# Weight tiles on GpSimd's DMA queue, and a planner with new books for transfers

## The chip, the core and the metric

The kernel runs on one core of one Trainium2 chip. The metric is the device time of one execution in microseconds (us). The engines are named as in the profile: PE (TensorE, with PEld for its weight loads), DVE (VectorE), ACT (ScalarE), POOL (GpSimd) and SP (SyncE, which here only issues transfers).

## The reference

A delta-rule attention (4 batches, 8 heads, 768 positions, head size 48), and then a gated FFN over its output (3072 tokens of 384, inner size 1536), all in float32. The weights arrive as 8-byte floats.

```python
k_n = k / (np.linalg.norm(k, axis=-1, keepdims=True) + 1e-06)
for t in range(S):
    kt, vt, bt = (k_n[:, :, t], v[:, :, t], beta[:, :, t, None])
    y[:, :, t] = np.einsum('bhd,bhde->bhe', q[:, :, t], state)
    v_old = np.einsum('bhde,bhd->bhe', state, kt)
    state = state + bt[:, :, :, None] * np.einsum('bhd,bhe->bhde', kt, vt - v_old)
...
xn = x / np.sqrt(np.mean(x * x, axis=-1, keepdims=True) + 1e-06) * rms_g
g = xn @ w_gate
out = (g * (1.0 / (1.0 + np.exp(-g))) * (xn @ w_val)) @ w_out
```

## The kernel before, in words

The 768 positions are cut into 12 chunks of 64. For every chunk, `prep` works out what the chunk needs of k and beta alone, `recur` applies and updates the state and gives the chunk's 256 normalized tokens, and an FFN follows.

`prep(c)` normalizes k (`norms`: the squares' sum on DVE, its square root on POOL at L538), forms the products of keys on PE (L516), copies them negated, writes them to a DRAM scratch `dkk`, and reads them back in another layout as `at` (256 KB in two halves). A triangular solve follows on DVE: 15 steps of a multiply (L682) and a reduce (L688). Its result goes through the DRAM scratch `dx` to the tiles `mt`, `x2bd` and `m1bd`, from which two small merges on PE (L764, L788) make the chunk's inverse. For chunks 0 and 1, PE turns a part of it (L740), and ACT (L751) and DVE (L753) each copy one half into `m1bd`. There is one `at` tile, so a chunk's `at` is loaded only when the solve before has read it. In `recur(c)`, PE applies the inverse (L875), the scores (L889) and the state update (L926); POOL takes a root for the RMS norm (L976); PE transposes the tokens (L997) and ACT writes them to `xf` (L1001).

Chunks 0 and 1 use a plain FFN in two halves (L1064 up, L1046 down), chunks 2 to 11 one with fewer products (L1157 up, L1214 down), whose factors DVE works out from the weights (L1122, L1193).

The weights are 18 tiles of 768 KB. Each is loaded as raw 8-byte numbers into one of three `raw` buffers (in tile `more`). ACT splits it (L454, L455) into one of two scratch pairs, and DVE joins the parts (L456, L457) into float32 in `w_in` or `wo_sb`. The first nine tiles feed the first half of the plain FFN.

The order of the work is not written out by hand. Every piece is handed to a class `Plan` as an `Op`: engine, estimated duration, priority, what it reads and writes, PSUM banks that it takes or frees. `Plan.run` makes 60 rounds: `forward` lists the pieces by their earliest possible start, and by key among equals, and reckons when each ends; `backward` works out from the end how late each could start, and that is the next round's key, slightly shaken. The best round by the reckoned end is emitted, so each engine gets its instructions in that fixed order. In the first 70 us of the plan, gaps on PE are filled with matmuls on the identity (L1314), which compute nothing.

A transfer in the plan (`dma`, from L367, its queue chosen at L368) occupies its issuing engine for `dur`, then one common server for `work`, 0.9 us after the issue at the earliest, and its user may start 0.7 us after that. `after` gives a time before which the plan does not issue it: the first seven weight tiles have one each (7.5, 5.0, 19.2, 27.2, 24.5, 33.3, 47.0), the others 48.8; the beta loads 7.5; the chunk 1 `at` 41.2; q, k and v have their own. Nearly all transfers are issued by SP; for chunk 0 some of them by ACT. L369 is the line of every issue.

Of the kernel before, what the change touches and what calls it, by code (L numbers as in the profile page):

```python
# [18 lines left out]
C = 64  # L19
# [9 lines left out]
SHAKE = 0.12  # L29


class Op:
    def __init__(self, eng, dur, fn, prio, deps, lat, acquire, release, slack):
# [4 lines left out]
        self.ready, self.dma, self.ahead, self.work = 0.0, False, 0.0, 0.0  # L38

# [23 lines left out]
class Plan:  # L63
# [47 lines left out]
    def forward(self, banks, until):  # L111

        at = dict.fromkeys(ENGINES, 0.0)
# [9 lines left out]
        order, server, end_, mode = [], 0.0, 0.0, 0  # L123
        backlog = 0.0
        while len(order) < len(self.ops):
            best = None
            for e in ENGINES:
                for op in cand[e]:
                    s = max(op.at, at[e])
                    if op.port:  # L130
                        s = max(s, held["POOL" if e == "DVE" else "DVE"])
# [23 lines left out]
            end = s + op.dur  # L155
# [17 lines left out]
            if op.dma:  # L173
                server = max(end + 0.9, server) + op.work
                end = server
# [8 lines left out]
        return order  # L184

# [64 lines left out]
def kernel(  # L250
# [116 lines left out]
    def dma(dst, src, prio, r=(), w=(), work=0.3, dur=0.5, eng="SP", after=0.0):  # L367
        queue = nc.scalar if eng == "ACT" else nc.sync  # L368
        op = P.add(eng, dur, lambda: queue.dma_start(out=dst, in_=src), prio, r, w, lat=0.7)  # L369
        op.dma, op.work, op.ready = True, work, after  # L370
# [44 lines left out]
    def load_small():  # L415
        for i in range(8):
            src = beta.rearrange("b (y g) (c i t) -> i g (b y) c t", i=2, g=2, t=W)[i // 2 % 2, i % 2]
            dma(beta_b[16 * i : 16 * i + 16], src, 0.5, w=[("beta", i)], work=0.2, after=7.5)
        dma(g_sb, moe_rms_g.rearrange("(t p) -> p t", p=128), 1, w=["g"], after=8.0)
# [6 lines left out]
    def weights():  # L426
# [14 lines left out]
        for n, (dst, src, keys) in enumerate(todo):  # L441
# [4 lines left out]
            dma(rdst, src, (0.1 if n == 0 else 3 + 2 * n), w=[("raw", i)], dur=0.7, work=3.06, after=(7.5, 5.0, 19.2, 27.2, 24.5, 33.3, 47.0)[n] if n < 7 else 48.8)  # L446
# [18 lines left out]
    def load(c, what):  # L465
        t0 = c * C
        pk, pq, pv = ((-5, 1, 12), (5, 29, 36))[c] if c < 2 else (due(c, 150), due(c, 99), due(c, 70))
        if "q" in what and c > 1:
            for d, eh, g, th in itertools.product(range(2), repeat=4):
# [3 lines left out]
                dma(q2t[r0 : r0 + 32, :, g, th, 0 : e1 - e0], src, pq, w=[q2k[8 * d + 4 * eh + 2 * g + th]], work=0.2, after=53.2)  # L473
        for key, t, src, pr in (("k2", k2[c % NK], k, pk), ("q2", q2, q, pq)):
            for g in range(2):
# [4 lines left out]
                dma(dst, s, pr, w=[(key, c % NK, g)] if key == "k2" else q2k[8 * g : 8 * g + 8], dur=0.7, work=1.02, eng="ACT" if c == 0 and g and key == "k2" else "SP", after=((0.0, 1.4, 0.0), (8.6, 27.2, 0.0))[c]["kqv".index(key[0])] if c < 2 else 53.2)  # L480
        if "v" in what:
            for bb in range(2):
                s = v[2 * bb : 2 * bb + 2, :, t0 : t0 + C, :].rearrange("p h t e -> t (p h) e")
                dma(vt[64 * bb : 64 * bb + 64], s, pv, w=[("v", bb)], dur=0.85, work=1.02, after=(34.4, 41.2)[c] if c < 2 else 60.0)
# [865 lines left out]
```

## Time and profile before

| what | us |
|---|---|
| median of 3 runs (717.48 to 721.77) | 720.96 |
| the profiled execution | 718.33 |
| its span, first to last instruction | 716.6 |
| PE busy (98% of the span) | 700.2 |
| filler matmuls among it (L1314) | 56.6 |
| DVE busy (74%) | 533.4 |
| ACT busy (44%) | 314.0 |
| POOL busy (19%) | 137.5 |

The transfers moved 54.66 MB. Nearly all went through one hardware queue (q1, that of SP: 52.27 MB), a small part through q10 (0.92 MB). Shares of the chain that ended last: PE 77%, DVE 10%, DMA 5%, SP's issuing 4%.

In a row of a group, "x164 | 56.6, 498 | 1.4" reads: 164 instructions, busy 56.6 us, 498 ns each on average, 1.4 us of idle time of the engine ahead of them. In a row of a timeline, the first number is the start and the second the duration; an issue on SP ("SPq") is the time that the issue took, not the transfer. A row of transfers gives the size of each and the median time from issue to landing.

### The profile page before, as it was taken

The numbers are of one execution on the slowest core, as the hardware profiler recorded it, in microseconds if no ns is written. First come the engines' busy times: TensorE is split into PE (matmuls) and PEld (weight loads), VectorE is DVE, ScalarE is ACT, GpSimd is POOL, SyncE is SP. The second block draws the span as 40 slices with busy tenths as digits, with TensorE's granted clock in tenths as the row PEclk, the third lists the DMA queues.
The fourth block names the chain that finished last, engine by engine and source line by source line (L and its number), as shares of the span: only waits on it lengthen the run. The fifth ranks groups of instructions, "written<-read, shape, count | busy, mean of one in ns | idle before, by whom it ended". The sixth has DMA issues, their size and how long they took to land.

```text
span 716.6 us, 23156 instructions
## 1 busy us (share of the span) xinstructions
PE 700.2 (98%) x9940; PEld 631.0 (88%) x9940; DVE 533.4 (74%) x1115; ACT 314.0 (44%) x724; POOL 137.5 (19%) x140
## 2 busy tenths in 40 slices
PE   8999799999999999999999999989999999999997
PEld 6655676777879999999999999989999999999997
DVE  4799549999349959959869888569859838947363
ACT  5454855323314534544545336424535345236231
POOL 4200203103031231322134304032133112000000
PEclk9999999999999999999999999999999999999999
DMA  7977887351531452531541634421551350040000
GB/s 139 240 173 188 188 228 127 53 86 29 85 67 27 84 96 42 90 54 22 94 74 30 102 58 65 72 52 25 76 96 19 47 97 2 13 65 2 23 1 23
DMA packets 232790, 54.66 MB, mean 76 GB/s; under 512 B 221936, under 2 KB 225008, under 8 KB 232688
## 3 DMA queue, kind: packets, MB, share of 16 engines
q1 hardware_dynamic: 227840, 52.27, 38.3%
q8 instruction: 78, 1.28, 0.8%
q10 hardware_dynamic: 4848, 0.92, 0.7%
q14 instruction: 24, 0.20, 0.1%
HBM read 40.83 MB, written 12.32 MB: 74 GB/s over the span
## 4 chain that ended last, share of the span: by engine, by line
PE 77%; DVE 10%; DMA 5%; SPq 4%; issue 2%; ACT 1%; POOL 1%; DVEq 0%; POOLq 0%; ACTq 0%
PE bank L1157 35%; PE bank L1214 17%; PE bank L1064 7%; SPq L369 4%; PE bank L1046 3%; DVE acc L688 3%; PE bank L516 3%; PE bank L829 3%; DMA more<-in_moe_w_out_dram 2%; DVE acc L682 2%; PE bank L875 2%; PE bank L788 2%; PE bank L889 2%; DVE tmp L1167 1%; PE bank L493 1%
## 5 line engine op out<-in xcount | busy, mean ns | idle before, releaser
L1157 PE MATMUL bank<-xf,w_in 128*128 128x128 f32 x1440 | 181.1, 277 | 0.0
L1157 PEld LDWEIGHTS bank<-xf,w_in 128*128 128x128 f32 x1440 | 170.1, 192 | 2.0 <-issue 0.6
L1167 DVE TENSOR_TENSOR tmp<-tmp,bank 128x512 f32<-128x512 f32 x180 | 120.7, 682 | 66.1 <-PE bank L1157 58.0
L1157 PE MATMUL bank<-xf,more 128*128 128x128 f32 x960 | 126.2, 279 | 2.0 <-DVE tmp L1167 2.0
L1157 PEld LDWEIGHTS bank<-xf,more 128*128 128x128 f32 x960 | 116.0, 193 | 4.7 <-DVE tmp L1167 2.4
L1169 ACT COPY tmp<-bank 128x512 f32<-128x512 f32 x120 | 68.9, 585 | 104.8 <-PE bank L1157 80.8
L688 DVE TENSOR_REDUCE acc<-acc 128x30 f32<-128x90 f32 (+4 forms) x180 | 85.0, 472 | 6.2
L1173 ACT ACTIVATE tmp<-tmp 128x256 f32<-128x256 f32 x120 | 49.6, 416 | 89.1 <-DVE tmp L1167 89.0
L538 POOL TENSOR_TENSOR knrm<-ksum,half 128x16 f32<-128x16 f32 x12 | 35.3, 2943 | 212.1 <-DVE ksum L537 212.1
L682 DVE TENSOR_TENSOR acc<-acc,at 128x60 f32<-128x60 f32 (+4 forms) x180 | 62.8, 349 | 8.8 <-DMA out_dram<-tmp 3.4
L1214 PE MATMUL bank<-wo_sb,hf 128*128 128x192 f32 x360 | 63.7, 327 | 0.0
L1214 PEld LDWEIGHTS bank<-wo_sb,hf 128*128 128x128 f32 x360 | 58.3, 190 | 0.1
L1314 PE MATMUL bank<-ident 128*128 128x512 f32 (+2 forms) x164 | 56.6, 498 | 1.4 <-POOL ident masks.py:199 1.4
L1174 DVE TENSOR_TENSOR hf<-tmp 128x256 f32<-128x256 f32 x120 | 50.5, 437 | 7.7 <-ACT tmp L1173 7.2
L1314 PEld LDWEIGHTS bank<-ident 128*128 128x128 f32 x164 | 29.7, 200 | 27.0 <-issue 24.7
L635 POOL TENSOR_TENSOR at<-at,beta_b 128x1024 f32<-128x1024 f32 x8 | 18.9, 2358 | 121.3 <-DMA at<-dkk 63.1
L709 POOL COPY acc<-acc 128x128 f32<-128x128 f32 x40 | 20.1, 532 | 89.8 <-DVE acc L688 89.6
L1223 DVE TENSOR_TENSOR tmp<-tmp,bank 128x192 f32<-128x192 f32 x30 | 10.5, 351 | 33.2 <-PE bank L1214 33.2
L1064 PE MATMUL bank<-xf,w_in 128*128 128x256 f32 x144 | 33.6, 385 | 0.0
L1064 PE MATMUL bank<-xp,w_in 128*128 128x256 f32 x144 | 33.5, 384 | 0.0
L1046 PE MATMUL bank<-wo_sb,hf 128*128 128x384 f32 x96 | 33.0, 488 | 0.0
L1064 PEld LDWEIGHTS bank<-xf,w_in 128*128 128x128 f32 x144 | 26.7, 190 | 4.5 <-issue 0.4
(156 smaller groups left out, 1000.3 us busy)
## 6 DMA issues: line engine op xcount, KB each, us to landing
at<-dkk SPq DMA_DIRECT2D x23, 256.0 KB, 4.1
more<-in_moe_w_val_dram SPq DMA_DIRECT2D x6, 768.0 KB, 7.2
more<-in_moe_w_gate_dram SPq DMA_DIRECT2D x6, 768.0 KB, 7.8
more<-in_moe_w_out_dram SPq DMA_DIRECT2D x6, 768.0 KB, 8.9
vt<-in_v_dram SPq DMA_DIRECT2D x24, 192.0 KB, 4.3
out_dram<-tmp SPq DMA_DIRECT2D x48, 96.0 KB, 2.2
k<-in_k_dram SPq DMA_DIRECT2D x23, 192.0 KB, 3.9
mt<-dx SPq DMA_DIRECT2D x84, 32.0 KB, 2.1
```

The costliest lines, as they stand in the source:

```text
L538: P.add("POOL", 2.95, lambda: nc.gpsimd.tensor_tensor(out=knrm[i2], in0=ksum[i2], in1=half, op=ALU.pow), pn, r=[("ksum", i2), "half"], w=[ ...
L682: nc.vector.tensor_tensor(out=acc[:, 1:3, 0:n, j + 2 : W].rearrange("p a i t -> p i a t"), in0=acc[:, old, 0:n, j : j + 2, None].to_broadc ...
L688: nc.vector.tensor_reduce(out=acc[:, new, 0:n, j + 2 : W], in_=acc[:, lo : lo + 3, 0:n, j + 2 : W].rearrange("p a i t -> p i t a"), axis=A ...
L1046: nc.tensor.matmul(po[p].t[:, 0:DM], hf[:, spot(f), 128 * p : 128 * p + 128], wo_sb[:, spot(f)], start=(f == f0), stop=(f == f1 - 1), skip ...
L1064: nc.tensor.matmul(ps.t[:, TOK * side : TOK * side + TOK], w_in[:, side, h_, 3 * t + i_, n : n + 128], x_[:, 2 * t : 2 * t + 2].rearrange( ...
L1157: nc.tensor.matmul(g.t[:, 128 * z : 128 * z + 128], fac[:, side, 128 * f : 128 * f + 128], xf[:, xs], start=(begin and z == 0), stop=False ...
L1167: P.add("DVE", V(512), lambda t=t, g=g: nc.vector.tensor_tensor(out=t, in0=t, in1=g.t, op=ALU.add), -1, r=[g], w=[tk], last=g)
L1169: P.add("ACT", A(512), lambda t=t, g=g: nc.scalar.copy(t, g.t), -1, r=[g], w=[tk], last=g)
L1173: P.add("ACT", A(256), lambda t=t: nc.scalar.activation(out=t[:, 0:256], in_=t[:, 0:256], func=ACTF.Silu), -1, w=[tk])
L1174: P.add("DVE", V(256), lambda t=t, f0=f0, p=p: nc.vector.tensor_tensor(out=hf[:, spot(f0) : spot(f0) + 2, 128 * p : 128 * p + 128], in0=t[ ...
L1214: nc.tensor.matmul(g.t[:, 0:192], a_[:, f], b_[:, f], start=(begin and f == 0), stop=(f == 5), skip_group_check=True)
L1314: nc.tensor.matmul(warm[:, 0 : 128 * w_].rearrange("p (w n) -> p w n", n=128), ident, ident[:, None, :].to_broadcast([128, w_, 128]))
```

## The change

Three things change in `dma`, in its calls, and in `Plan`. The kernel's arithmetic, tiles and buffers stay.

1. The 18 weight loads are issued on POOL's queue, not on SP's.
2. All `after` times of transfers are gone. A load of q and k for chunks 2 and later, and of v for chunks 1 and later, is marked `hold`: the plan does not issue it more than 24 us before its key.
3. `forward` reckons otherwise. POOL's transfers have a server of their own, starting 1.08 us after the issue and landing 0.9 us after the server is done. Those of SP and ACT share the other one, 1.08 us after the start of the issue, and are stretched by up to 0.6 of their work while POOL's server is busy, which is pushed back as well. A transfer is not issued before the eighth one ahead of it on its kind of queue has landed. An issue on SP or ACT also ends only when its descriptors (`desc`) fit with those still under way into a room of 2330 (`room`). The estimates of `dur` and `work` are new throughout.

```diff
+RING, LANES, FIRST, LAND = 2330, 8, 1.08, 0.9
+HOLD = 24.0
...
                     s = max(op.at, at[e])
+                    if op.dma:
+                        s = max(s, (softly if op.soft else landed)[-LANES])
+                        if op.held:
+                            s = max(s, op.key - HOLD)
...
-            if op.dma:
-                server = max(end + 0.9, server) + op.work
-                end = server
+            if op.soft:
+                soft = max(end + FIRST, soft) + op.work
+                end = soft + LAND
+                softly.append(end)
+            elif op.dma:
+                end = self.room(sent, end, op.desc)
+                at[op.eng] = end
+                begun = max(server, s + FIRST)
+                work = op.work
+                if soft > begun:
+                    work += min(0.6 * op.work, soft - begun)
+                    soft += op.work
+                server = max(begun + work, end)
+                sent.append((begun, server, op.desc))
+                end = server + LAND
+                landed.append(end)
...
+    def room(self, sent, t, desc):
+
+        left = lambda t: sum(n if t <= a else n * (b - t) / (b - a) for a, b, n in sent[-24:] if b > t) + desc
+        if left(t) <= RING:
+            return t
+        lo, hi = t, max(b for a, b, n in sent[-24:])
+        for _ in range(12):
+            mid = (lo + hi) / 2
+            lo, hi = (mid, hi) if left(mid) > RING else (lo, mid)
+        return hi
...
-    def dma(dst, src, prio, r=(), w=(), work=0.3, dur=0.5, eng="SP", after=0.0):
-        queue = nc.scalar if eng == "ACT" else nc.sync
-        op = P.add(eng, dur, lambda: queue.dma_start(out=dst, in_=src), prio, r, w, lat=0.7)
-        op.dma, op.work, op.ready = True, work, after
+    def dma(dst, src, prio, r=(), w=(), work=0.2, dur=0.45, eng="SP", after=0.0, desc=256, hold=False):
+        queue = {"ACT": nc.scalar, "SP": nc.sync, "POOL": nc.gpsimd}[eng]
+        op = P.add(eng, dur, lambda: queue.dma_start(out=dst, in_=src), prio, r, w, lat=0.1)
+        op.dma, op.work, op.ready, op.desc, op.soft, op.held = True, work, after, desc, eng == "POOL", hold
+        op.port = False
...
-            dma(rdst, src, (0.1 if n == 0 else 3 + 2 * n), w=[("raw", i)], dur=0.7, work=3.06, after=(7.5, 5.0, 19.2, 27.2, 24.5, 33.3, 47.0)[n] if n < 7 else 48.8)
+            dma(rdst, src, (0.1 if n == 0 else 3 + 2 * n), w=[("raw", i)], dur=1.3, work=3.06, eng="POOL")
```

The other calls only lose `after` and get other estimates, for instance the two halves of `at`:

```diff
-                dk.rearrange("i g x j t -> (i g x) (j t)"), pd, r=dkeys, w=[("at", par)], dur=0.56, work=1.8, eng="SP" if par or c else "ACT", after=41.2 if c == 1 else 0.0)
+                dk.rearrange("i g x j t -> (i g x) (j t)"), pd, r=dkeys, w=[("at", par)], dur=0.5, work=1.42, desc=64, eng="SP" if par or c else "ACT")
```

## The prediction

> **What bounds the kernel now.** I read the page's first two parts, then the busy time by stretch, then in the first 90 us the chain of work that ended last, the timelines of PE, DVE, ACT and POOL, and the SP issues with their landings. The page first:
>
> ```profile
> PE 700.2 (98%) x9940; PEld 631.0 (88%) x9940; DVE 533.4 (74%) x1115; ACT 314.0 (44%) x724; POOL 137.5 (19%) x140
> ...
> L1314 PE MATMUL bank<-ident 128*128 128x512 f32 (+2 forms) x164 | 56.6, 498 | 1.4 <-POOL ident masks.py:199 1.4
> ...
> at<-dkk SPq DMA_DIRECT2D x23, 256.0 KB, 4.1
> ```
>
> PE is busy in 700.2 of 716.6 us, so 16.4 are idle; but 56.6 of the busy time is L1314, the filler matmuls on `ident` that compute nothing. So some 73 us hold no useful PE work, and all but some 9 of them lie in the first 90 us. The busy time by stretch says where:
>
> ```profile
> 60.00:70.00 10.00, 8.40 (x70) 5.35 (x69) 9.14 (x20) 5.81 (x10) 0.00 (x0) 0.86 0.71 146
> 70.00:80.00 10.00, 7.55 (x273) 7.01 (x272) 7.52 (x16) 8.15 (x24) 5.88 (x4) 0.84 0.89 215
> ...
> 280.00:330.00 50.00, 50.00 (x651) 48.62 (x652) 39.63 (x89) 22.77 (x55) 16.57 (x14) 1.00 0.34 60
> ...
> 430.00:480.00 50.00, 48.42 (x700) 46.63 (x698) 33.03 (x71) 23.99 (x58) 13.45 (x13) 1.00 0.39 67
> ```
>
> The columns are stretch, length, busy PE, PEld, DVE, ACT and POOL, then granted clock, DMA share and GB/s. From 230 to 680 us PE idles 0 to 1.58 us in 50, 3.3 in all; the end (680 to 717) adds 4.5. Past the start there is little to win. The start ends with the first useful FFN matmul (L1064), at 84.19 on PE's timeline. What it waits for, on the chain of work that ended last:
>
> ```profile
> 17.55 7.50 DMA at<-dkk
> ...
> 43.36 3.22 DMA dx<-wsum
> ...
> 64.60 0.28 DVE acc L688
> 64.88 0.32 DVE m1bd L753
> ```
>
> and on the timelines of ACT and DVE (start, duration):
>
> ```profile
> 54.96 0.73 ACT L751 COPY m1bd<-bank 32x256 f32<-32x256 f32 x2 [1.63 <-PE bank L740]
> ```
>
> ```profile
> 48.29 1.22 DVE L635 TENSOR_TENSOR at<-at,beta_b 128x1024 f32<-128x1024 f32 x1
> ...
> 64.79 0.84 DVE L753 COPY m1bd<-bank 32x256 f32<-32x256 f32 x2
> ```
>
> ACT copies its half of chunk 0's m1bd at 54.96; DVE copies the other half at 64.79, since chunk 1's whole solve (48.29 to 64.8) stands ahead of it in DVE's order. That is 9.8 us of the wait for the FFN, put there by the planner. The `at` load (17.55, 7.50 us against a median of 4.1) is the other visible stretch. On SP the weight loads are in the way:
>
> ```profile
> 31.54 4.79 SPq L369 DMA_DIRECT2D more<-in_moe_w_gate_dram  x1
> ...
> 57.14 4.75 SPq L369 DMA_DIRECT2D more<-in_moe_w_gate_dram  x1
> ```
>
> **The change part by part.** The profiled execution took 718.33 us (span 716.6, 1.73 around it); the median shown, 720.96, is 2.63 above. The sum goes against 718.33.
>
> *Eighteen weight issues leave SP.* Their durations on SP's timeline add up to 28.9 us, from 0.37 to 5.73 each. On SP they delayed others: chunk 1's dx was issued at 71.50, its mt only from 82.26. None of that ends PE's wait: with FFN work of chunk 0 at hand PE is busy from 84 to 114. What covers it is that first FFN half; without that cover chunk 1 would lead and the freed SP would gain more. Counted at 0.
>
> *The same issues land on POOL.* No DMA of POOL is in this trace. An issue is bounded by 0.37 (quickest on SP) and 2.94 (mean of L538, POOL's longest frequent instruction); I take the 1.3 that the diff books, which lies between. 18 x 1.3 = 23.4 us, beside 23.3 us of POOL work in the first 120 us: room enough on average. On the path lie L538 at 70.87 and the two L976 at 74.45 and 76.09, whose rs chunk 0's output waits for; three weight issues fell between 69 and 78 us. One issue ahead of rs costs 1.3, two 2.6, none 0. I take +1.3. An issue also waits until its `raw` buffer is free, with POOL's queue behind it: that is a rival.
>
> *`at` without a weight ahead on its own queue.* Its SP half took 7.50 behind a gate tile issued at 16.52. Its ACT half, issued at 17.46 with no weight on its queue, took 6.00 beside the same traffic. Best is the median 4.1 (-3.4); worst the pair issued at 100.00 and 100.80 with three weights in flight, 11.31 (+3.8). I take the ACT half, the same load at the same time: -1.5. It carries through, as DVE is 92% busy from 30 to 70. The Trainium skill, "DMA: Bandwidth & Descriptors", section "Issuing engines are not separate DMA queues", says that transfers of all issuers share the same 16 engines and that several issuers save only issue time; by it this term would be 0 and the sum 713.3. The 6.00 against 7.50 speaks for a part of it, not for none.
>
> *The planner's new books and the fixed release times gone.* This re-draws the order of all engines. Costs per small transfer hardly change: the old plan counts 0.5 + 0.9 + 0.3 + 0.7 = 2.4 from issue to use, the new one 1.08 + 0.2 + 0.9 + 0.1 = 2.28; the trace's median for mt is 2.1. What changes is the start, where weights no longer sit in the same line and chunk 1's `at` is no longer held to 41.2. So the one order that I cost is m1bd against chunk 1's solve. Kept: 0. Turned: DVE copies after at most one step (L682 and L688, 1.0), so 9.8 - 1.0 = -8.8. Worse: another whole solve in front, +16.4. I take -8.8: m1bd is chunk 0's and everything on PE waits for it, and the solve loses only the 0.84 of the copies. What is then late next: PE did other chunks' work in the wait before 84.19 (L516, L493, L516: 1.55 + 1.97 + 1.42 = 4.9 us). If the FFN comes sooner, part of that falls behind it: 0 to +4.9, I take +2.5. The granted clock of 0.84 to 0.86 between 60 and 80 also costs: L493 takes 1.97 at 78.38 against 1.04 at 126.98. If PE's pauses shrink, up to 0.9 comes back, if they grow as much is lost; 0.
>
> *The steady part re-planned,* with held loads, eight lanes and room. Bounds: all nine 50 us windows like the best, -3.3; all like the worst, 9 x 1.58 - 3.3 = +11. The old costs and the new are nearly equal there: 0.
>
> *Release times of the first loads.* k and q go first anyway (0.79 to 3.84); the beta loads, last landed at 17.71, are used at 17.89 (L607); late by as much as the slowest of them (5.33 against 2.35) they would cost 3, early 0.6 of idle time saved; 0.
>
> Sum: 718.33 + 1.3 - 1.5 - 8.8 + 2.5 = **711.8 us**.
>
> **The rivals.**
> *Order kept.* m1bd stays behind the solve: 718.33 + 1.3 - 1.5 = 718.1. For it: the old plan chose that order with DVE as its scarce engine (92% from 30 to 70, 95% from 110 to 180). Against: with `at` of chunk 1 free to move, the two no longer meet where they did.
>
> *DVE starves the issues.* If POOL cannot issue while DVE works, the four tiles converted from 41.7 to 48.3 (L456 and L457, 0.55 + 0.96 each) come after chunk 1's solve and stand ahead of chunk 0's copies: +6.0, 717.8. The trace has no overlap of the kind; L538 took 2.92 with DVE idle and 3.14 at 70.87 with DVE busy. The Trainium skill, "SBUF — State Buffer", sections "SBUF: two separate sides" and "Who interferes with whom", says that a GpSimd-issued transfer cannot have its descriptors written while VectorE holds the shared ports in a two-port mode, and names tensor_scalar and copies, not the two-input and reduce forms. By it only L456 (0.55) stands in the way of an issue, two of them ahead of rs: the sum would be 712.9. No run so far shows it.
>
> *POOL's queue stands (slower).* Place: a weight issue ahead of L976 or L538, waiting for ACT to have read the `raw` buffer. Price: SP's own such waits, 5.6 (xf L454) and 4.0 at the longest (more L455), together 9.6; with the order kept, 718.1 + 9.6 = 727.7. It decides from a wait of 6.5 on, which is what the forecast gains. For it: POOL runs in order, and POOL had nothing that waited on ACT's conversions before. Against: POOL's work is sparse before 70 us, so few issues have a critical instruction right behind.
>
> *All of chunk 0's path freed.* `at` at its median (-3.4), dx from 4.87 to the 3.5 of dx<-acc (-1.4), m1bd at once (-9.8), clock loss gone (-0.9), no issue ahead of rs: 702.8.
>
> **How the numbers follow.** Forecast (706 to 717) 0.42; freed path 0.12; order kept or starved issues 0.22, of which 0.08 starved; POOL stands, or the steady part at its bad end (718.33 + 11 = 729), 0.24. Within 1%, which is about what a measurement can tell from no change, means 713.8 to 728.2 against 720.96. Three quarters of the forecast's chance (0.31) and the freed path make faster 0.43; the forecast's rest 0.11, the second group 0.22 and a sixth of the last, 0.04, make same 0.37; slower 0.20. The range takes in the freed path and the bad steady part: 702 to 729. The likeliest case alone: 706 to 717.
>
> **What would show it.** Right: L1064 first runs near 76 to 78; m1bd L753 within 2 us of ACT's L751; `at` of chunk 0 lands in about 6 us; L1314 under 50 us; no issue over 2 us on SP before 110. A POOL issue near 1.3, and no wait of L976 above 1.5. Wrong: L753 still behind a solve's last L688; POOL's L976 or L538 idle behind a DMA issue; idle PE of more than 3 us in a 50 us window after 230; or the filler time growing.

## The result, and the profile after

The change makes the kernel slower: 743.62 us (median of 4 runs, 740.76 to 746.01) against 721.37 us for the kernel before in the same comparison (4 runs, 717.48 to 724.17), a ratio of 1.0311, 95% interval [1.0248, 1.0373]. The forecast was 711.8 us, its range 702 to 729.

In the changed file the lines below `dma` have moved: an issue is L402 (was L369), ACT's and DVE's conversions are L488 to L491 (L454 to L457), PE's turn is L774 (L740), m1bd is copied at L785 and L787 (L751, L753), the solve is L716 and L722 (L682, L688), the merges are L798 and L822 (L764, L788), the root for the RMS norm is L1010 (L976), FFN up is L1098 (L1064), and the filler is L1348 (L1314).

From the first and the fifth part of the page after:

```profile
PE 705.3 (95%) x9938; PEld 635.6 (86%) x9938; DVE 536.0 (72%) x1115; ACT 315.1 (42%) x724; POOL 151.8 (20%) x158
...
L1348 PE MATMUL bank<-ident 128*128 128x512 f32 (+2 forms) x162 | 55.7, 497 | 1.4 <-POOL ident masks.py:199 1.4
```

The profiled execution has a span of 743.0 us, 26.4 more than before. PE's idle time is 743.0 - 705.3 = 37.7 us against 16.4: +21.3. The filler shrank by 0.9. PE's other work, the same matmuls, took 705.3 - 55.7 = 649.6 against 643.6: +6.0, at a mean granted clock of 0.981 against 0.992. These three make up the 26.4. By place, PE idles 20.0 us before the first FFN matmul (before: 7.5), 2.8 from there to 230 us (1.6), 10.6 from 230 to 680 (3.2) and 4.3 at the end (4.1). The busy time by stretch, with the columns as before:

```profile
60.00:70.00 10.00, 3.47 (x12) 1.90 (x10) 9.11 (x21) 1.63 (x2) 1.52 (x2) 0.79 0.98 264
70.00:80.00 10.00, 9.92 (x118) 6.19 (x120) 3.77 (x8) 1.10 (x3) 0.00 (x0) 0.69 0.18 33
...
90.00:100.00 10.00, 6.52 (x51) 4.74 (x52) 6.47 (x10) 9.66 (x22) 3.13 (x4) 0.66 0.87 185
...
230.00:280.00 50.00, 46.64 (x884) 44.70 (x883) 40.75 (x83) 21.12 (x49) 7.49 (x8) 0.97 0.30 52
280.00:330.00 50.00, 49.14 (x815) 47.53 (x814) 39.24 (x87) 23.32 (x57) 11.77 (x11) 1.00 0.36 58
...
430.00:480.00 50.00, 50.00 (x818) 48.39 (x817) 43.18 (x91) 22.20 (x52) 11.06 (x12) 1.00 0.45 76
```

From 60 to 70 PE is busy for 3.47 us where it was busy for 8.40. What it waits for stands on PE's timeline (start, duration, and in brackets the idle time ahead and what ended it), and the FFN starts at 93.78, 9.6 us later than before:

```profile
70.08 1.74 PE L774 MATMUL bank<-ident,mt 32*32 32x32 f32 x64 [6.61 <-DMA mt<-dx]
71.75 6.93 PE L1348 MATMUL bank<-ident 128*128 128x512 f32 x14
...
93.78 5.49 PE L1098 MATMUL bank<-xf,w_in 128*128 128x256 f32 x12 [3.48 <-ACT xf L1035]
```

The last row shows the price of a pause: 12 matmuls in 5.49 us, while before a run of 12 of the same took 2.86; the granted clock from 90 to 100 is 0.66. PE's timeline before:

```profile
91.90 2.86 PE L1064 MATMUL bank<-xf,w_in 128*128 128x256 f32 x12
```

The second row of the timeline after is filler, 6.93 us of it, and the next useful matmul (L798) starts only at 78.61, though both copies of m1bd that it reads are done by 72.60 (shown below). So up to 6.0 us of the late start are filler that stands in PE's fixed order; no run tested this by itself. On the chain that ended last, the start lost time at three places:

```profile
10.72 10.61 DMA q<-in_q_dram
...
37.76 1.23 DVE at L669
...
60.63 9.31 DMA mt<-dx
```

Chunk 0's q is issued at 10.07 and 10.72, behind beta and chunk 1's k, and its second half takes 10.61 us to land; before it was issued at 1.62 and 2.57. Chunk 0's solve begins at 37.76, before at 25.14. Its mt takes 9.31 us. Both transfers run beside weights, which now have nothing that holds them back. SP's timeline before, with q and the first two weights, and the start of the solve on the chain of before:

```profile
1.62 2.21 SPq L369 DMA_DIRECT2D q<-in_q_dram  x2
3.88 0.83 SPq L369 DMA_DIRECT2D more<-in_moe_w_val_dram  x1
...
16.52 0.38 SPq L369 DMA_DIRECT2D more<-in_moe_w_gate_dram  x1
```

```profile
25.14 1.24 DVE at L635
```

POOL's timeline after has the weights' issues:

```profile
2.21 1.01 POOL L402 DMA_DIRECT2D more<-in_moe_w_val_dram  x1
...
5.83 1.53 POOL L402 DMA_DIRECT2D more<-in_moe_w_gate_dram  x2
...
58.66 0.72 POOL L402 DMA_DIRECT2D more<-in_moe_w_out_dram  x1 [17.91 <-ACT more L489]
60.30 0.76 POOL L402 DMA_DIRECT2D more<-in_moe_w_gate_dram  x1 [0.91 <-ACT tmp L489]
61.93 0.76 POOL L402 DMA_DIRECT2D more<-in_moe_w_val_dram  x1 [0.87 <-ACT more L489]
86.01 1.74 POOL L1010 TENSOR_TENSOR rs<-ms,mhalf 128x1 f32<-128x1 f32 x2 [23.33 <-DVE ms L1003]
```

Three weights were in the air by 6.6 us; before it was one, at 3.88, and the next at 16.52. Three more were issued at 58.66 to 61.93, right when chunk 0's mt and x2bd were (60.22 to 64). The transfers of the first 30 us, sizes and median time to landing, before and after:

```profile
q<-in_q_dram SPq DMA_DIRECT2D x3, 192.0 KB, 4.8
...
beta_b<-in_beta_dram SPq DMA_DIRECT2D x8, 24.0 KB, 4.1
```

```profile
q<-in_q_dram SPq DMA_DIRECT2D x4, 192.0 KB, 6.2
...
beta_b<-in_beta_dram SPq DMA_DIRECT2D x8, 24.0 KB, 8.3
```

Beta took twice the time. It delays more than its own user: ACT, whose order is fixed, waited for it until 17.04 and 17.72, and ACT's two dkk issues stand behind that (the first at 17.82, before at 13.79). SP's two stand behind q, v and g (20.98, before 13.79). The `at` loads wait for all four, and come at 24.93 and 27.43 where they were at 17.55 and 17.46. They land by 31.11, before by 25.05.

That is 6.1 us of the 12.6 by which the solve begins later. The other 6.6, from 31.11 to 37.76, are order: DVE has a conversion of a weight (L490) ahead of the solve, which waits for ACT's part of it (L488), and ACT has the copies of chunk 1's turned q (35.38) ahead of that. On the chain, PE's work up to that turn runs without a pause from the landing of chunk 0's late q at 21.33, and 5.8 us of it are filler. ACT's timeline, then DVE's:

```profile
36.34 0.92 ACT L488 ACTIVATE xf<-more 128x768 f32<-128x768 f32 x1
```

```profile
37.29 0.56 DVE L490 TENSOR_SCALAR xf<-xf 128x768 uint32<-128x768 uint32 x1 [3.30 <-ACT xf L488]
37.76 1.22 DVE L669 TENSOR_TENSOR at<-at,bk 128x1024 f32<-128x1024 f32 x1
```

The m1bd copies did turn, as forecast. DVE's half comes inside chunk 1's solve, and ahead of ACT's (ACT's timeline, then DVE's):

```profile
71.86 0.74 ACT L785 COPY m1bd<-bank 32x256 f32<-32x256 f32 x2 [10.24 <-DMA mt<-dx]
```

```profile
71.18 0.85 DVE L787 COPY m1bd<-bank 32x256 f32<-32x256 f32 x2 [1.45 <-PE bank L774]
```

### The profile page after: what moved, and what is told of

Read it like the earlier page. It is cut to its first block, busy times and chain, and to the rows that moved or that the text cites. A ratio compares the mean times of both kernels' runs of the same rounds, so it can differ in the third digit from the quotient of the medians.

```text
span 743.0 us, 23208 instructions
## 1 busy us (share of the span) xinstructions
PE 705.3 (95%) x9938; PEld 635.6 (86%) x9938; DVE 536.0 (72%) x1115; ACT 315.1 (42%) x724; POOL 151.8 (20%) x158
## 4 chain that ended last, share of the span: by engine, by line
PE 69%; DVE 10%; DMA 8%; SPq 6%; ACT 3%; POOL 3%; issue 2%; ACTq 0%; DVEq 0%; POOLq 0%
PE bank L1191 27%; PE bank L1248 16%; PE bank L1098 8%; SPq L402 6%; PE bank L1080 3%; PE bank L550 2%; PE bank L863 2%; PE bank L1348 2%; DMA q<-in_q_dram 2%; DVE acc L722 2%; PE bank L527 2%; DMA mt<-dx 2%; DVE acc L716 1%; DVE tmp L1201 1%; DMA out_dram<-tmp 1%
## 5 line engine op out<-in xcount | busy, mean ns | idle before, releaser
L1191 PEld LDWEIGHTS bank<-xf,w_in 128*128 128x128 f32 x1440 | 170.8, 193 | 6.9 <-ACT tmp L1203 3.5
L1203 ACT COPY tmp<-bank 128x512 f32<-128x512 f32 x120 | 68.9, 584 | 89.5 <-PE bank L1191 65.7
L722 DVE TENSOR_REDUCE acc<-acc 128x30 f32<-128x90 f32 (+4 forms) x180 | 85.0, 472 | 6.2
L716 DVE TENSOR_TENSOR acc<-acc,at 128x60 f32<-128x60 f32 (+4 forms) x180 | 64.2, 356 | 10.0 <-POOL at L699 7.0
L1208 DVE TENSOR_TENSOR hf<-tmp 128x256 f32<-128x256 f32 x120 | 54.2, 467 | 11.7 <-ACT tmp L1207 10.7
L1348 PE MATMUL bank<-ident 128*128 128x512 f32 (+2 forms) x162 | 55.7, 497 | 1.4 <-POOL ident masks.py:199 1.4
L572 POOL TENSOR_TENSOR knrm<-ksum,half 128x16 f32<-128x16 f32 x12 | 36.6, 3052 | 85.5 <-DVE ksum L571 85.5
L1348 PEld LDWEIGHTS bank<-ident 128*128 128x128 f32 x162 | 29.8, 204 | 25.9 <-issue 23.4
L743 POOL COPY acc<-acc 128x128 f32<-128x128 f32 x40 | 17.1, 457 | 143.4 <-DVE acc L722 142.6
L1098 PE MATMUL bank<-xf,w_in 128*128 128x256 f32 x144 | 36.8, 408 | 3.5 <-ACT xf L1035 3.5
L1098 PEld LDWEIGHTS bank<-xf,w_in 128*128 128x128 f32 x144 | 28.3, 202 | 8.9 <-ACT xf L1035 3.7
L1098 PE MATMUL bank<-xp,w_in 128*128 128x256 f32 x144 | 33.1, 383 | 0.0
L1098 PEld LDWEIGHTS bank<-xp,w_in 128*128 128x128 f32 x144 | 26.9, 190 | 4.3
```

The costliest lines, as they stand in the source:

```text
L716: nc.vector.tensor_tensor(out=acc[:, 1:3, 0:n, j + 2 : W].rearrange("p a i t -> p i a t"), in0=acc[:, old, 0:n, j : j + 2, None].to_broadc ...
L722: nc.vector.tensor_reduce(out=acc[:, new, 0:n, j + 2 : W], in_=acc[:, lo : lo + 3, 0:n, j + 2 : W].rearrange("p a i t -> p i t a"), axis=A ...
L1098: nc.tensor.matmul(ps.t[:, TOK * side : TOK * side + TOK], w_in[:, side, h_, 3 * t + i_, n : n + 128], x_[:, 2 * t : 2 * t + 2].rearrange( ...
L1191: nc.tensor.matmul(g.t[:, 128 * z : 128 * z + 128], fac[:, side, 128 * f : 128 * f + 128], xf[:, xs], start=(begin and z == 0), stop=False ...
L1203: P.add("ACT", A(512), lambda t=t, g=g: nc.scalar.copy(t, g.t), -1, r=[g], w=[tk], last=g)
L1208: P.add("DVE", V(256), lambda t=t, f0=f0, p=p: nc.vector.tensor_tensor(out=hf[:, spot(f0) : spot(f0) + 2, 128 * p : 128 * p + 128], in0=t[ ...
```

## The experiments

The theories ("books" are the plan's reckoning of transfers). A: weights on POOL's queue take the DMA engines from the small transfers, whatever the order. B: the newly drawn order costs the time, not the queue. C: the release times had kept weights out of chunk 0's way, and their loss makes the start late (C1: those of the weights, C2: those of the small loads). D: the new books draw a poorer order for what follows the start. E: any new draw is worse than the one the kernel was left with. Two more came later: F, that the copy behind chunk 1's solve is worth the 8.8 us less 2.5 of the forecast, and G, that an earlier FFN is given back.

All runs of the whole kernel, each with its ratio to the kernel before on the same chip, whose median there was between 718.12 and 721.37; medians of different rows are therefore compared with care. "FFN" is the start of the first useful FFN matmul, "rest" the span after it, both of the profiled execution; "idle" is PE's idle time before the FFN, from there to 230, and from 230 to 680 us. In oldbooks_no_release the filler is only 20.0 us, so more of the wait shows as idle time.

| run | median us | ratio | FFN | rest | idle |
|---|---|---|---|---|---|
| before | 721.37 | 1 | 84.2 | 632.4 | 7.5, 1.6, 3.2 |
| after | 743.62 | 1.0311 [1.0248, 1.0373] | 93.8 | 649.2 | 20.0, 2.8, 10.6 |
| oldplan_pool | 717.15 | 0.9981 [0.9948, 1.0014] | 82.3 | 635.0 | 7.0, 2.1, 3.6 |
| newplan_sp | 740.83 | 1.0338 [1.0295, 1.0380] | 89.7 | 647.7 | 15.3, 3.3, 8.0 |
| gate_mt | 732.26 | 1.0232 [1.0176, 1.0289] | 83.8 | 645.7 | 11.3, 7.3, 4.3 |
| oldbooks_no_release | 735.08 | 1.0230 [1.0185, 1.0275] | 98.6 | 633.4 | 54.5, 2.8, 0.0 |
| newbooks_release | 725.74 | 1.0099 [1.0062, 1.0136] | 75.4 | 648.6 | 6.5, 10.3, 3.5 |
| newplan_seed1 | 730.34 | 1.0175 [1.0125, 1.0224] | 91.9 | 636.4 | 10.9, 2.7, 4.9 |
| oldplan_seed1 | 716.66 | 0.9957 [0.9932, 0.9982] | 84.7 | 631.7 | 8.3, 2.1, 3.0 |
| release_weights | 728.36 | 1.0110 [1.0066, 1.0154] | 85.2 | 640.2 | 10.2, 5.5, 5.9 |
| release_small | 750.81 | 1.0398 [1.0339, 1.0456] | 92.2 | 656.7 | 11.7, 7.8, 13.9 |
| newbooks_release_seed1 | 719.24 | 1.0003 [0.9972, 1.0034] | 85.7 | 633.2 | 10.0, 1.7, 4.7 |
| newbooks_release_seed2 | 728.02 | 1.0089 [1.0058, 1.0120] | 75.8 | 651.2 | 8.1, 14.6, 3.6 |
| m1bd_act | 717.61 | 0.9978 [0.9948, 1.0008] | 82.8 | 635.0 | 10.1, 1.2, 3.2 |
| m1bd_act_seed1 | 716.74 | 0.9962 [0.9939, 0.9986] | 79.0 | 636.0 | 7.6, 2.8, 3.4 |
| m1bd_act_release | 732.75 | 1.0196 [1.0149, 1.0243] | 82.7 | 647.3 | 7.1, 11.0, 5.5 |
| oldplan_pool_seed1 | 713.36 | 0.9911 [0.9880, 0.9941] | 82.5 | 630.0 | 7.2, 1.0, 2.7 |
| chunk0_act_seed1 | 711.10 | 0.9915 [0.9888, 0.9942] | 72.8 | 636.9 | 3.7, 4.9, 1.8 |
| chunk0_act_pool_seed1 | 711.78 | 0.9920 [0.9892, 0.9947] | 75.6 | 630.6 | 5.8, 0.8, 2.6 |

### The queue alone, and the order alone

oldplan_pool keeps the plan of before and only emits the weight loads on POOL; newplan_sp keeps the plan of after and emits them on SP.

```diff
-            dma(rdst, src, ..., dur=0.7, work=3.06, after=(7.5, ...)[n] if n < 7 else 48.8)
+            dma(rdst, src, ..., dur=0.7, work=3.06, after=(7.5, ...)[n] if n < 7 else 48.8, on=nc.gpsimd)
```

```diff
-            dma(rdst, src, ..., dur=1.3, work=3.06, eng="POOL")
+            dma(rdst, src, ..., dur=1.3, work=3.06, eng="POOL", on=nc.sync)
```

> The old plan to the letter, only the queue on which the 18 weight loads are issued is POOL's, each in the place where the old order has it. Theory A (the queue: weights on POOL's queue starve the small transfers beside them, as mt of chunk 0 took 8 to 10 us in the changed kernel against 2 to 3 before): mt of chunk 0 or the beta loads land 5 us or more later where a weight is under way, the first FFN matmul comes 5 to 12 us after 84.2, the time is 727 to 735. Theory B (the re-drawn order is what costs): nothing of that, 714 to 724. If freeing SP is worth something by itself: below 716.

> The new plan to the letter, weights issued by SP in the place where the new order has them. Theory A: mt of chunk 0 lands within 3 us again, the first FFN matmul moves from 93.8 to 82 to 88, the time is 730 to 737. Theory B: the first FFN matmul stays past 91 and the time stays at 740 to 748, or is longer, as SP now waits with the weights for the raw buffers ahead of urgent small loads.

The queue alone changes nothing that can be measured (0.9981), the order alone the whole of it (1.0338). As the cause of the time theory A falls and B stands, though the FFN's start in newplan_sp, 89.7, lies between the bounds of the two. In newplan_sp chunk 0's mt took 4.5 to 6.1 us beside weights that SP itself had issued. In oldplan_pool its first loads did slow down, to 7.2 to 7.4 us beside two weights of POOL (before: 2.8 to 3.1), but that was hidden: DVE's half of m1bd still stands behind chunk 1's solve there, at 62.81, and the turn on PE that needs mt had begun at 54.38.

### Small transfers beside large ones

transfers_alone computes nothing of the reference and writes zeros. It issues the eight loads of mt's shape, or the two of a k tile, on SP, alone or with three weight tiles issued just before on POOL, ACT or SP.

```python
weights(queue)
...
small(nc.sync)
```

> No part of the reference is computed; the output is zeros. Eight mt-shaped loads (32 KB in runs of 128 bytes) and then the two loads of a chunk's k (192 KB in runs of 192 bytes) are issued on SP alone, beside three weight tiles on POOL's queue, beside three on ACT's, and behind three on SP's own; and the mt loads beside weights on POOL cut into runs of 512 bytes. Theory A: mt alone 2.1 us each, beside POOL 8 to 10, beside ACT at most 5; cut into 512 bytes about halfway back. Rival (any other queue does the same, it is the shared engines): ACT as slow as POOL. Rival (not the transfers but the plan): beside POOL under 4.

Largely inconclusive: the memsets between took longer than thought, so most of the small loads were issued when the weights were nearly done. The few that met one weight, issued 0.1 to 0.8 us ahead of them, say this much: a 32 KB load that takes 1.6 to 2.3 us alone took 4.86 and 4.71 us behind POOL's weights of 109.10 and 131.84, and 4.62, 4.31, 4.85 and 4.55 behind ACT's of 29.25 and 120.20. One more, 0.35 us behind POOL's weight of 18.16, took 2.02, so not every such load is slowed. In these few the issuer makes no difference that shows. Of the 192 KB loads of k, which take 3.2 to 4.0 us alone, those that a weight followed within 1.0 us took 7.07 and 6.44 (ACT's weight) and 4.85 (SP's own). Neither three in the air nor the weights in runs of 512 bytes met a small load.

### Holding three weights back

gate_mt is the kernel after, but the three weights that it issues at 58.66 to 61.93 are emitted behind two tiny copies on POOL that read chunk 0's mt and x2bd, so they start when these have landed.

```diff
+            if op.tag == "w" and any(lo < s < hi for _, _, lo, hi, _ in GATES):
+                held.append(op)
+            else:
+                op.fn()
...
+                if mine and s > ahead and seen.get(tag, 0) == count:
+                    self.gate(tag)
```

> The changed kernel, with one thing more: the three weights that were issued at 58.7, 60.3 and 61.9 are issued only when POOL has read one element of each part of chunk 0's mt and x2bd (two tiny copies ahead of them on POOL). Theory A: mt and x2bd land by 65 (they landed by 74.2), PE's turn of chunk 0 (70.1) comes 5 to 7 us sooner, the first FFN matmul at 86 to 90, the time 5 to 8 us shorter than 743.6. Theory B: mt lands sooner, but fillers and DVE's fixed order take it back: less than 2 us.

The transfers of mt in the kernel after, 58 to 75 us, and in gate_mt, 50 to 66 us:

```profile
mt<-dx SPq DMA_DIRECT2D x4, 32.0 KB, 7.7
mt<-dx ACTq DMA_DIRECT2D x4, 32.0 KB, 4.7
```

```profile
mt<-dx SPq DMA_DIRECT2D x4, 32.0 KB, 2.2
mt<-dx ACTq DMA_DIRECT2D x4, 32.0 KB, 2.4
```

The same loads with the weights away take 2.2 to 2.4 us. PE's timeline in gate_mt has the turn, which reads mt, and the first FFN matmuls:

```profile
61.09 1.11 PE L786 MATMUL bank<-ident,mt 32*32 32x32 f32 x64
...
83.78 4.54 PE L1110 MATMUL bank<-xf,w_in 128*128 128x256 f32 x12 [3.48 <-ACT xf L1047]
```

The turn starts at 61.09 in place of 70.08 (2.3 of it from a solve that began sooner, at 35.5), and the FFN at 83.8 in place of 93.8. So most of what the start had lost hung on these three weights. In time it is less sharp: the median falls by 11 us (743.62 to 732.26), but one of the four runs took 739.18, and by the ratios, 1.0311 and 1.0232, it is some 6 us with intervals that overlap. The rest of the span keeps its loss (645.7).

### The release times

oldbooks_no_release is the kernel before with all release times at 0. newbooks_release is the kernel after with all of them put back; release_weights has those of the weights alone, release_small those of the others alone.

```diff
-        op.dma, op.work, op.ready = True, work, after
+        op.dma, op.work, op.ready = True, work, 0.0
```

```diff
-            dma(rdst, src, ..., dur=1.3, work=3.06, eng="POOL")
+            dma(rdst, src, ..., dur=1.3, work=3.06, eng="POOL", after=(7.5, 5.0, 19.2, 27.2, 24.5, 33.3, 47.0)[n] if n < 7 else 48.8)
...
-            dma(beta_b[16 * i : 16 * i + 16], src, 0.5, w=[("beta", i)], work=0.1, desc=192)
+            dma(beta_b[16 * i : 16 * i + 16], src, 0.5, w=[("beta", i)], work=0.1, desc=192, after=7.5)
```

> The kernel before with one thing taken out: all release times of transfers (`after`) are 0; books and queue are the old ones, the plan is drawn anew. Theory C (the release times kept weights and later loads out of the way of chunk 0's small transfers; without them the plan issues them too early): first FFN matmul 5 to 12 us later, 728 to 742. Theory D (the new books are what draws the poor plan): 714 to 724. Theory E (any re-drawn plan is worse than the one in hand): anywhere from 715 to 740, with nothing to see in the loads.

> The changed kernel with the old release times put back on every transfer; new books, weights planned and issued on POOL, holds kept. Theory C: the solve of chunk 0 starts by 27 again (37.8 in the changed kernel), first FFN matmul by 86, 718 to 728. Theory D: the solve starts past 32 or the rest after the first FFN matmul stays 10 us longer than before; 733 to 748. Theory E: anywhere.

> The kernel after, with the old release times put back on the 18 weight loads alone (the first seven from 5.0 to 47.0, all later ones from 48.8 in the planner's time); beta, q, k, v and chunk 1's at stay without. Theory C1: what the start lost is chunk 0's small transfers running beside weights, so the weights' times alone carry it: the first useful FFN matmul falls from 93.8 us to between 74 and 84 us, chunk 0's solve starts before 28 us (37.8 after, 26.1 with all release times), and the time is 723 to 735 us. Theory C2: the other release times carry it (beta and v issued early stand in front of what chunk 0 needs): the solve still starts after 33 us, the FFN after 90 us, the time is 738 us or more.

> The kernel after, with the old release times put back on beta, g, q, k, v and chunk 1's at, and none on the weight loads: the complement of the run on the weights alone. Theory C1: the weights still lie beside chunk 0's loads, so the start stays late (solve of chunk 0 after 33 us, FFN after 88 us) and the time is 735 to 750 us. Theory C2: the start comes back (solve before 28 us, FFN before 84 us), 723 to 735 us.

Without release times the old books lose 15.6 us (735.08 against 719.49), all of it at the start: the solve of chunk 0 begins at 38.4, near the 37.8 of the kernel after, the FFN at 98.6, and the rest is the old one (633.4). What ends the solve's wait there is not `at` either, but a weight that the plan takes early: it lands, ACT and DVE convert it, and the solve stands behind. On the chain that ended last:

```profile
26.68 9.00 DMA more<-in_moe_w_gate_dram
...
35.77 0.89 ACT more L454
...
37.48 0.04 DVE w_in L457
...
38.35 1.23 DVE at L635
```

The release times on the weights alone bring the kernel after from 743.62 to 728.36; the solve starts at 29.2 and the FFN at 85.2, 1.2 us past the bound that C1 had set for each. Those on the small loads alone bring nothing (750.81, 0.8 past C1's bound): q is issued at 1.64 and 2.56 again, but beside three weights its second half takes 12.79 us. C1 stands. What is left of the late start in release_weights is again weights beside loads of chunk 0; on its chain:

```profile
19.82 9.33 DMA at<-dkk
...
51.78 8.88 DMA mt<-dx
```

Two weights were issued on POOL at 14.50 and 16.74, ahead of that `at`, with two loads of q at 16.86 and 17.57 beside them, and three weights at 50.08 to 52.05, around that mt. With all release times back (newbooks_release) the start is better than before: 75.4.

### The draw

Four runs change only the seed of the planner's shaking.

```diff
-        rng = random.Random(47)
+        rng = random.Random(1)
```

> The changed kernel with another seed (1 for 47) for the small shakes of the keys between rounds, nothing else. Theories C and D: the same weaknesses, 733 to 750. Theory E: it can come out near 720 as well as 750.

> The kernel before with seed 1 for 47, nothing else. Theories C and D: 714 to 726. Theory E: 725 to 745, as the plan of before was one good draw.

> The kernel after with all old release times, and another random draw of the planner's order (seed 1 in place of 47). With seed 47 the FFN began at 75.4 us (before: 84.2) and what follows took 648.6 us (before: 632.4). Theory D (the new books choose a poorer order for what follows the start, whatever the draw): the part after the first FFN matmul takes 642 us or more and the time is over 718 us. Theory of the draw (seed 47 was unlucky): that part takes 632 to 638 us behind a start of 75 to 80 us, 708 to 719 us, which would beat the kernel before.

> As the run with seed 1, with seed 2: a third draw under the new books with the old release times. Theory D: 642 us or more from the first FFN matmul to the end. Theory of the draw: 632 to 638 us in one of the two at least, and a time of 708 to 719 us.

A new draw of the old plan is not worse (0.9957), so E falls. Under the new books the draws lie far apart: 743.62 and 730.34 without release times, 725.74, 719.24 and 728.02 with them. The best of the five only reaches the kernel before. As every edit of the planner is also a new draw, one pair would not do for the release times; three pairs that differ in them alone agree: 15.6 us in the old books, 17.9 in the new (743.62 to 725.74), 11.1 in the new with seed 1 (730.34 to 719.24). D does not hold for every draw (newbooks_release_seed1 has a rest of 633.2 behind an FFN at 85.7), and the other expectation, a rest of 632 to 638 behind a start of 75 to 80, fell too: both draws with an early FFN, 75.4 and 75.8, pay 16 to 19 us in the rest, and PE idles 10.3 and 14.6 us between the FFN's start and 230. PE's timeline in newbooks_release shows where:

```profile
75.42 5.35 PE L1098 MATMUL bank<-xf,w_in 128*128 128x256 f32 x24
...
87.04 1.95 PE L863 MATMUL bank<-state,kt 48*64 48x48 f32 x60 [5.09 <-ACT acc L674]
88.92 6.55 PE L1098 MATMUL bank<-xf,w_in 128*128 128x256 f32 x24
```

PE waits 5.09 us for ACT, which in its order waits for chunk 1's solve. That solve ran from 68.9 to 85.5, because the first half of chunk 1's `at` landed only at 67.48 (before: both by 48.08), because its dkk writes were issued from 54.68 on, behind chunk 0's mt (before: from 26.62, long ahead of it). DVE stood nearly idle meanwhile, 2.92 us busy from 50 to 60. After the wait the granted clock is down to 0.72 (80 to 90) and 0.84 (90 to 110). In newbooks_release_seed2 the dkk writes go at 55.13, with the same poor rest; in newbooks_release_seed1 they go at 28.24, and the rest is the old one. So in these draws what was won for chunk 0 was taken from chunk 1; this is read from three traces, and no run changed the place of the dkk writes alone.

### The copy behind the solve

m1bd_act is the kernel before with DVE's half of m1bd given to ACT; m1bd_act_seed1 the same with seed 1; m1bd_act_release is newbooks_release_seed1 with this edit.

```diff
-                    if bb:
+                    if True:
                         P.add("ACT", A(256), lambda dst=dst, f=src: nc.scalar.copy(dst, f()), pi, r=[psm[bb]], w=[("m1bd", g, bb)], last=psm[bb])
```

> The kernel before with one edit: the half of m1bd that DVE copied (L753) goes to ACT like the other half, so chunk 1's solve on DVE no longer stands ahead of it; the planner draws anew. Theory F (the prediction's step: the copy behind the solve is worth 8.8 us, less 2.5 for work that then falls behind): the first useful FFN matmul at 74 to 78 us instead of 84.2, the part after it 632 to 637 us, and the time 709 to 715 us, ratio below 0.993. Theory G (the solve of chunk 1 costs PE the same wherever it stands; an early FFN start is given back): FFN earlier by 5 us or more but the part after it longer by as much, idle PE between the FFN's start and 230 us up from 1.6 to 6 us or more, time 717 to 724 us.

> As m1bd_act, with the planner's other draw (seed 1), so that one draw does not decide. Theory F: 709 to 715 us with an FFN start before 78 us. Theory G: 716 to 724 us, with the idle PE time after the FFN's start grown by what the start won.

> The kernel after with the old release times, seed 1, and both halves of m1bd copied by ACT. Without that edit this draw took 718.9 us of span, with the FFN at 85.7 and 633.2 us after it. Theory F: FFN at 76 to 79 us and 633 to 638 us after it, 711 to 716 us of time. Theory G: the sum of the two parts stays at 717 us or more.

Neither F nor G as written. All four m1bd copies are done by 53.3 in m1bd_act, 12 us sooner than before, but the FFN starts only 1.4 us sooner, and 5.7 in the other draw (79.0 against 84.7). What is late next is another copy of chunk 0: DVE's half of mt. ACT's timeline and DVE's, in m1bd_act:

```profile
55.48 0.58 ACT L802 COPY mt<-bank 32x512 f32<-32x512 f32 x1 [1.27 <-PE bank L788]
```

```profile
68.09 0.67 DVE L804 COPY mt<-bank 32x512 f32<-32x512 f32 x1
```

ACT's half is copied at 55.48, DVE's at 68.09, near the end of the same solve. m1bd_act_release drew another poor rest (647.3, idle 11.0 from the FFN to 230) and says nothing on this.

chunk0_act_seed1 takes both copies off DVE, in the kernel before with seed 1; chunk0_act_pool_seed1 also emits the weights on POOL. oldplan_pool_seed1 has the queue and the seed alone.

```diff
-            if c or bb:
+            if True:
                 P.add("ACT", A(512), lambda dst=dst, s=src: nc.scalar.copy(dst, s()), pi, r=[ps2[bb]], w=[("mt", imt, 2, bb)], last=ps2[bb])
```

> The plan of the kernel before drawn with seed 1, its weight loads emitted on GpSimd's queue; nothing else. Each part alone gave a ratio of 0.9957 [0.9932, 0.9982] (the draw) and 0.9981 [0.9948, 1.0014] (the queue). If they add: 0.994, about 715 us. If the queue is worth nothing and the draw's gain is its own: 0.996. If the draw's gain hung on the landings that it was drawn for: 1.000.

> The kernel before, drawn with seed 1, with two edits: ACT copies both halves of m1bd and both halves of chunk 0's mt, so DVE has none of chunk 0's copies between its two solves. Theory F2 (the copies are worth what the prediction said once the next one is out of the way as well): FFN at 72 to 77 us where the same draw without the edits has 84.7, and 709 to 713 us, a ratio of 0.985 to 0.992. Theory G (an earlier FFN is given back): FFN earlier by 5 us or more, the part after it longer by nearly as much, and the time within 0.4% of the draw alone, a ratio of 0.992 to 1.000.

> The same with the weight loads emitted on GpSimd's queue. That queue with this draw and DVE's copies gave a ratio of 0.9911 [0.988, 0.9941]. Theory F2: 0.978 to 0.987. Theory G: 0.988 to 0.995.

oldplan_pool_seed1, at 0.9911, came out a little below what adding the two parts would give (0.994), which its interval still takes in. With both copies away PE reaches the FFN at 72.79:

```profile
71.06 0.87 PE L997 MATMUL bank<-ident,yn 128*128 128x128 f32 x6
72.79 2.86 PE L1064 MATMUL bank<-xf,w_in 128*128 128x256 f32 x12 [0.85 <-ACT xf L1001]
```

That is 11.9 us before the same draw without the edits (84.7); 5.2 come back in the rest (636.9 against 631.7), and the profiled span is 709.7 against 716.4, -6.7 us. By the ratios, 0.9957 to 0.9915, it is 0.0042, some 3 us, and the two intervals overlap by 0.001. F2, which is F with the second copy out of the way too, met its three bounds, at the upper edge of the ratio's. With the weights on POOL as well it did not: the edits brought nothing to the ratio (0.9911 without, 0.9920 with, inside G's bounds of 0.988 to 0.995), though the profiled spans are 712.5 and 706.2, the latter from the fastest of 12 runs (707.88 to 716.40). So the size of this step lies between 0 and 6.7 us and is not settled closer. All three runs beat both kernels, by 0.8 to 0.9% against before.

## Why the prediction was wrong, point by point

**Release times of the first loads, counted 0: the step that failed.** It said that k and q go first anyway and priced only beta, by 3 at most. In the new plan q did not go first (10.07 where it was 1.62). And the step looked at the small loads' times, while it was those of the weights that mattered: they decide what runs beside every small load of chunk 0, and how early the weights' conversions stand in the order of ACT and DVE. The loss of all release times costs the old books 15.6 us (oldbooks_no_release), and putting the weights' back won 15.3 (743.62 to 728.36), the small loads' none (release_small). Behind the step stands another sentence of the prediction, that costs per small transfer hardly change. It held the books against the median of mt, 2.1 us, and not against what mt takes beside weights. The new books lengthen a load beside a weight by at most 0.6 of its own work, 0.12 us for mt; the runs show 5.5 (SP's mt, 7.7 against 2.2).

**`at` without a weight on its own queue, -1.5: wrong sign.** The flight did get shorter, 4.43 and 3.69 us against 7.50 and 6.00. But the issue came 7.4 and 10.0 later, behind beta on ACT and behind q and v on SP; it landed 6.1 us later, and the solve did not even start then. And the reason given was wrong: in release_weights, with the weights on POOL, `at` on SP took 9.33 and the half on ACT 7.48; in oldplan_pool, with no weight in the air from 16.19 to 21.63, the halves took 4.61 and 4.76. What counts is what is in the air, more than whose queue it is on. The Trainium skill, "DMA: Bandwidth & Descriptors", section "Issuing engines are not separate DMA queues", says that transfers started by any engine run on the same 16 DMA engines and interleave. The trace agrees (7.48 on ACT beside POOL's weights, 7.50 on SP behind SP's own).

**Eighteen issues off SP, 0: right.** oldplan_pool, 0.9981 [0.9948, 1.0014]. That no issue on SP would take over 2 us was wrong: the second of q took 5.01, at 10.72.

**The issues on POOL, +1.3: too much.** An issue took 0.72 to 0.81 us, the first 1.01, and none stood ahead of rs: rs at 86.01 waited for DVE, and POOL's last issue was at 61.93. The rival in which POOL's queue stands had its waits, up to 17.91 us for a `raw` buffer, but no critical instruction behind them. The rival in which DVE starves the issues fell as well: those at 38.37 and 39.99, with DVE in its solve, took 0.72 and 0.76 us. The Trainium skill, "SBUF — State Buffer", section "Who interferes with whom", holds that two-port forms of VectorE keep such an issue waiting; no run here shows it.

**The planner turns the m1bd copy, -8.8 + 2.5: the turn was right, its value was not.** It came, in the kernel after too (71.18, 0.7 us ahead of ACT's half), but behind a chunk 0 that was already late. With the release times back (newbooks_release) the FFN did start 8.8 us sooner, at 75.4, but chunk 1 was late next and the rest grew by 16.2. In the old books "what is then late next" had been answered too shortly as well: DVE's copy of mt stands behind the same solve, and only with both copies away did the start gain 11.9 us, 5.2 of them given back. The moved work was 4.4 us in newbooks_release (useful PE work before the FFN 84.2 - 7.5 - 56.6 = 20.1 before, 75.4 - 6.5 - 53.2 = 15.7 there), inside the bounds of 0 to 4.9.

**The steady part, 0: too low.** The span after the FFN's start grew by 16.8 us: 8.8 of idle time (1.2 up to 230, 7.4 from there to 680, 0.2 at the end), 2.0 of other work that moved behind the FFN's start (useful PE work ahead of it, in busy time: 18.1 against 20.1), and 6.0 of the same matmuls taking longer, where the mean clock alone would give 643.6 x (0.992 / 0.981 - 1) = 7.2, an estimate. The idle 3.36 us from 230 to 280 are one of the signs that the prediction had named for being wrong. The 7.4 lie inside the bound of +11 and come from the draw in part: the same books with seed 1 idle 4.9 there. Which of the new books (held loads, lanes, room, or the costs) draws the poorer orders was not tried.

## What to carry to other kernels

A fixed release time in a planner may look arbitrary and still be what keeps bulk loads from running beside the few small loads that start the critical chain: before dropping one, list what will be in the air next to each of those loads. A bulk transfer moved to another engine's queue can still slow the small loads (7.2 to 7.4 us for mt in oldplan_pool), so ask when it starts before you ask who issues it. Hold a planner's price for two transfers side by side against a trace: 0.12 us was booked here, 5.5 measured. Work that a plan places early, the conversion of a weight or filler, keeps its place in its engine's order when the plan runs late, and then stands in front of the critical chain. When one copy is moved out from behind a long solve, look for the next instruction of the same chain on the same engine; it waits behind the same solve.

## What the runs showed of the hardware

A small load's time hangs mainly on what is in the air with it. In release_weights the beta loads of 24 KB issued up to 6.18 took 2.3 to 3.1 us, those from 6.66 on, behind the first weight (5.68), 5.0 to 5.4; in the kernel after, with three weights out, up to 10.84. A 32 KB load takes 2.2 us with no weight in the air, 4.3 to 4.9 just behind one (2.0 in one case of seven), 7.5 to 10.1 beside three. In the kernel after, an issue of a 768 KB weight took 0.72 to 0.81 us on POOL, the first 1.01; on SP, before, the same issue took 0.37 to 5.73. Around pauses of 3.5 to 6.6 us on PE the granted clock was 0.66 to 0.79 in a stretch of 10 us, and 12 FFN matmuls behind one of 3.48 us took 5.49 us in place of 2.86. The Trainium skill, "TensorE: Matmul & The Clock Gate", part 1, says that the array falls to half its clock after an idle window of about 3.4 us and is back after as long a busy one. The trace agrees on the fall (1.92 times as long); the granted clock was 0.50 until 100.0 here, 6.2 us after PE had started again.
